# First chunk: slots for all eight q/k tiles, and their transposes in one run behind gate/up group 2

## The chip, the core and the metric

The kernel runs on one core of one Trainium2 chip. A core has a matrix engine (PE, with its weight loads shown as PEld), a vector engine (DVE), a scalar engine (ACT), GpSimd (POOL) and a sync engine (SP), each with an instruction stream of its own, and 16 DMA engines that the streams feed. The metric is the device time of one execution in microseconds (us); lower is better. Before the change the median of three runs is 576.93 us.

## The reference

A sequence of 2048 tokens of width 576 in bf16. The normed input goes through sliding-window attention (32 heads of 18, a window of 256) and through a gated block (width 4608), and the two results are multiplied:

```python
xn = layernorm(x)
qkv = xn @ wqkv                    # 576 x 1728; 32 heads, Dh = 18
mask = (i - j >= 0) & (i - j < 256)
p = softmax(where(mask, q @ k.T * Dh ** -0.5, -1e9))
s = (p @ v).reshape(B, S, D) @ wo
h = sigmoid(xn @ w_gate) * (xn @ w_up)     # width F = 4608
g = silu(h @ w_down)
out = x + s * g
```

## The kernel before

The tokens are cut into four chunks of 512 (`NCH`, `CH`), each of four tiles of 128. A chunk goes through layer norm, the projections to q, k and v, attention interleaved with the gate/up product, the output projection of the attention, and the down projection. The program is built as a list of operations with dependencies; `schedule` (a planner with estimated durations, transfer sizes and priorities) fixes the order on each engine before anything runs, and `emit` writes that order out with semaphore waits. On the chip each engine, SP too, goes through its own list in order; an instruction that has to wait holds up all that stand behind it.

What matters here is the first chunk:

- Projections (`project`, line 448). One q, k or v tile of 128 tokens takes 18 matmuls; the chunk has twelve such tiles, created in the order of `QKV_FIRST` ("q0 q1 v0 v1 q2 v2 k0 v3 k1 q3 k2 k3").
- `build_qk`. A q or k tile is copied from PSUM (q by DVE at line 490, k by ACT at line 491) into one of `RPK` = 3 slots of the buffer `pk`, 32 heads padded to 32 columns each. The padding is zeroed once by `pkz` on ACT (line 323). From the slot a DMA transpose, issued by SP (line 205), puts the tile into `qkp`, from which the scores are computed. A slot is taken again only when its transpose has landed; eight tiles share three slots.
- Gate/up weights (`load9`, line 206). The 4608 columns are cut into 36 tiles and these into 12 groups of three; a group is four DMAs of 240, 192, 192 and 240 KB into one of `RW` = 3 buffers `wgs`. A tile takes 18 matmuls (line 748), a group 54. The buffer of a group is free for the third next one when its last matmul is done.
- Attention (`build_unit`, line 556 for the scores; `build_pv`, line 639). The scores go to PSUM banks 0 to 3, ACT writes their exponentials (line 579) into one of `NEXP` = 5 buffers `expr`, DVE masks them (line 611), and PV reads them. A unit of scores needs the transposed q and k tiles that it multiplies.
- `behind`: an operation with this mark is placed by the planner only after the named one has been placed. Before, the transposes from the third on (`QKT_BEHIND = 2`) stand behind the last DMA of gate/up group 1.

On SP this gives, in order: the x tiles, the weights of q and v, gate/up group 0, the weights of k, two transposes (q0, q1), group 1, one transpose (q2), group 2, two transposes (k0, k1), group 3, three transposes (q3, k2, k3), group 4, and so on. On PE: seven projection tiles, 26 gate/up matmuls, two projection tiles, 36 gate/up, one tile, 36 gate/up, two tiles, 8 gate/up, and the first unit of scores.

Of the kernel before, what the change touches and what calls it, by code (L numbers as in the profile page):

```python
# [10 lines left out]
DH = 18  # L11
F = 4608
P = 128
# [21 lines left out]
RW = 3  # L35
RT = 2
NEXP = 5
RPK = 3
HP = 32
# [31 lines left out]
LATE_SLACK = 5000.0  # L71
LN_STEP = 1
XT_CUT = 4
QKT_BEHIND = 2
WARM = 10
X0_SLACK = 0.0
X_PRIO = (-9, -9, -9, -9)
# [3 lines left out]
W_FACTOR = 1.42  # L81
X0_FACTOR = 1.7
XT_BYTES = 1.2
DMA_LAT_NS = 1600.0
DMA_BYTES_PER_NS = 320.0


def mm_ns(n):
    return max(28.0, n / 2.4 + 2.5)


def act_ns(n):
    return n / 1.2 + 80.0


def dve_ns(n, rate=1.0):
    return n / (0.96 * rate) + 75.0
# [68 lines left out]
class Builder:  # L166
# [16 lines left out]
    def op(self, eng, occ, fn, name, deps=(), prio=3, **kw):  # L183
        o = Op(eng, occ, fn, name, deps, prio, **kw)
        o.cidx = len(self.ops)
        self.ops.append(o)
        return o
# [117 lines left out]
    def build_init(self):  # L305
        op = self.op
        self.op_negh = op("DVE", 60, lambda e: e.memset(self.neghalf[:, :], -0.5), "neghalf", prio=0)
        self.op_pre = op("DVE", 250, lambda e: e.memset(self.hT[:, 0, :], 1.0), "pre", prio=-9)
        id1 = op("POOL", 200, lambda e: e.memset(self.op_[:, NOT - 1, 0:P], 1.0), "id1", prio=0)
        self.op_ident = op("POOL", 300, lambda e: e.affine_select(  # L310
            self.op_[:, NOT - 1, 0:P], self.op_[:, NOT - 1, 0:P], pattern=[[1, P]], compare_op=ALU.is_equal, fill=0.0,
            base=0, channel_multiplier=-1), "id2", deps=[id1], prio=0)
        m1 = op("POOL", 300, lambda e: e.memset(self.m13[:, :, :], 1.0), "m1", prio=1)
        m2 = op("POOL", 300, lambda e: e.affine_select(
            self.m13[:, 0, :], self.m13[:, 0, :], pattern=[[1, P]], compare_op=ALU.is_ge, fill=0.0,
            base=0, channel_multiplier=-1), "m2", deps=[m1], prio=1)
        self.op_mask = op("POOL", 300, lambda e: e.affine_select(
            self.m13[:, 1, :], self.m13[:, 1, :], pattern=[[-1, P]], compare_op=ALU.is_ge, fill=0.0,
            base=-1, channel_multiplier=1), "m3", deps=[m2], prio=1)
        vo1 = op("POOL", 1100, lambda e: e.memset(self.vau[:, :, 0:H, DH:DH + 1], 1.0), "vones", prio=1)  # L320
        self.op_vones = op("POOL", 300, lambda e: e.memset(self.vau[:, :, H, :], 1.0), "vpad", deps=[vo1], prio=1)
        self.warm(WARM, "warm:0", [self.op_pre])
        self.op_pkz = op("ACT", 1300 + 1900, lambda e: e.memzero(self.pk[:, :, :, :]), "pkz", prio=0)

    def warm(self, n, name, deps):
        ps = Psum((3,))
# [4 lines left out]
            return r  # L331
        self.op_warm = self.pe(n * WARM_NS, f, name, deps=deps, prio=-9, psum=[ps])

    def load9(self, low, up, w_low, w_up, name, lane, deps, prio, factor=1.42):
        cols = w_low.shape[1]
        a = w_low.rearrange("(j p) c -> p j c", p=64)
        b = w_up.rearrange("(j p) c -> p j c", p=64)
        out = []
        for k, (dst, src, n) in enumerate(((low[:, 0:5, :], a[:, 0:NC:2, :], 5), (up[:, 0:4, :], b[:, 1:NC:2, :], 4),
                                           (low[:, 5:NC, :], a[:, 1:NC:2, :], 4), (up[:, 4:NC, :], b[:, 0:NC:2, :], 5))):  # L340
            out.append(self.dma(dst, src, factor * n * 64 * cols * 2, f"{name}.{k}", lane + (k,), deps=deps, prio=prio,
                                issue=W_ISSUE_NS))
        return out
# [31 lines left out]
    def build_ln(self, c):  # L375
# [4 lines left out]
        for i in range(QPC):  # L380
# [30 lines left out]
            if c > 0:  # L411
                for k, (i0, i1, col) in enumerate(((0, NKT, 0), (NKT, NC, 64))):
                    o = self.dma(self.xn[:, i0:i1, tok], self.xnr[:, sr, col:col + (i1 - i0) * P],
                                 XT_BYTES * (i1 - i0) * P * P * 2, f"xt:{st}.{k}", ("xt", i, k), deps=[wr, ap] + dxn,
                                 prio=-2, issue=XT_ISSUE_NS, transpose=True)
# [65 lines left out]
            prev = o  # L481

    def build_qk(self, c, i, j, old):
        spk, dpk = self.r_pk.take()
        o, ps = self.project(c, i, j, f"qk:{c}:{i}:{j}", dpk, self.op_pv[c - 1][NHG - 1] if c > 0 else None)

        def f_ev(e):
            dst = self.pk[:, spk, :, 0:DH].rearrange("p (t h) d -> p t h d", t=2)
            if j == 0:
                return e.tensor_copy(dst, self.halves(ps))  # L490
            return e.activation(dst, self.halves(ps), ACTF.Copy)  # L491
        ev = self.rd("ACT" if j else "DVE", act_ns(D) if j else dve_ns(D), f_ev, f"qke:{c}:{i}:{j}",
                     deps=[o, self.op_pkz] + [t for t in (self.op_on[c - 1] if c > 0 else [])], prio=1, psum=[ps])
        c0 = j * CH + i * P
        dm = self.dma(self.qkp[:, :, c0:c0 + P], self.pk[:, spk, :, :].rearrange("p h d -> p (h d)"),
                      XT_BYTES * 8 * P * P * 2, f"qkt:{c}:{i}:{j}", ("qk", i, j), deps=[ev] + old, prio=0,
                      issue=XT_ISSUE_NS, transpose=True)
        self.r_pk.release(spk, dm)
        (self.op_q, self.op_k)[j].append(dm)
        self.op_qkt.append(dm)  # L500
        return o
# [223 lines left out]
    def build_ffn(self, c):  # L725
# [25 lines left out]
        for ft in range(NFT + 1):  # L751
            if ft < NFT:
                if ft % FG == 0:
                    fg = ft // FG
                    sw, dw = self.r_w.take()
                    slots.append(sw)
                    wp = W_PRIO[fg] if c == 0 and fg < RW else -2
                    fc = slice(fg * FG * P, (fg + 1) * FG * P)
                    ws = self.load9(self.wgs[0:64, sw, :, :], self.wgs[64:P, sw, :, :], self.wg[:, fc],
                                    self.wu[:, fc], f"w:{c}:{fg}", ("w", sw),  # L760
                                    dw + ([self.w_gate] if c > 0 and fg < RW else []), wp)
                    dmas.append(ws)
                    if c == 0 and fg == 1:
                        for o in self.op_qkt[QKT_BEHIND:]:
                            o.behind = ws[-1:]
                pg.append(Psum((6,), (7,), (5,), (4,)))
                pu.append(Psum((6,), (7,), (5,), (4,)))
            war = [self.f2_last[ft // WDG]] if self.f2_last and ft < NFT else []

            def f_a(e, ft=ft):  # L770
                for i in range(NA):
                    if ft < NFT:
                        r = step(e, 0, ft, i)
                    if ft > 0:
                        r = step(e, 1, ft - 1, NC - NA + i)
                return r
            oa = self.pe(NA * mm_ns(CH), f_a, f"fa:{c}:{ft}",
                         deps=(dmas[ft // FG] + self.all_xn + war if ft < NFT else []), prio=3,
                         psum=[pg[ft]] if ft < NFT else [], mode="r64", odeps=mms)
            if ft > 0:  # L780
                pu[ft - 1].users.append(oa)
                if ft % FG == 0:
                    self.r_w.release(slots[ft // FG - 1], oa)
                th_mul(ft - 1, ob, oa)
            if ft == NFT:
                break

            def f_b(e, ft, i0, i1):
                for i in range(i0, i1):
                    step(e, 0, ft, NA + i)  # L790
                    r = step(e, 1, ft, i)
                return r
            ob = oa
            for n, (i0, i1) in enumerate(zip(FB_CUTS, FB_CUTS[1:])):
                ob = self.pe((i1 - i0) * mm_ns(CH), lambda e, ft=ft, i0=i0, i1=i1: f_b(e, ft, i0, i1), f"fb{n}:{c}:{ft}",
                             deps=[ob], prio=3, psum=[pu[ft]] if n == 0 else [], mode="r64")
                if n > 0:
                    pu[ft].users.append(ob)
            pg[ft].users.append(ob)
            self.op_f1[(c, ft)] = ob  # L800
            mms = [ob]
# [5 lines left out]
        for blocks in (((0, 1), (2,), (3,)) if c == 0 else ((0,), (1,), (2,), (3,))):  # L807
# [5 lines left out]
            for q in range(NWD):  # L813
                for i in blocks:
                    def f_f2(e, q=q, i=i, ps=banks[i]):
                        b = ps.banks[0] * 512
                        for fl in range(WDG):
                            ft = q * WDG + fl
                            lhsT = self.hT[:, ft, i * P:(i + 1) * P]
                            for n0, n1 in ((0, 512), (512, D)):  # L820
# [3 lines left out]
                    deps = [self.op_hT[ft] for ft in range(q * WDG, (q + 1) * WDG)] + [self.op_wd[q]]  # L824
                    o = self.op("PE", WDG * (mm_ns(512) + mm_ns(64)), f_f2, f"f2:{c * QPC + i}:{q}", deps, 3,
                                alloc=[banks[i]] if q == 0 else [], mode="full",
                                odeps=prev + ([self.op_wop[i - RTH]] if q == 0 and i >= RTH else []))
# [66 lines left out]
    def schedule(self):  # L894
# [46 lines left out]
        while n < total:  # L941
# [37 lines left out]
            if o.lane is not None:  # L979
                free[e] = st + o.occ  # L980
                bs = max(free[e] + DMA_LAT_NS, bw)
                bw = bs + o.nbytes / DMA_BYTES_PER_NS
# [147 lines left out]
```

## Time and profile before

| | |
|---|---|
| median of three runs | 576.93 us (576.13 to 577.06) |
| the profiled execution | 576.29 us |
| its span, first to last instruction | 574.5 us |
| PE busy | 566.0 us (99%) |
| DVE, ACT, POOL busy | 294.1, 300.8, 23.0 us |
| granted clock of PE, mean | 0.998 |
| gate/up matmuls (line 748) | 298.7 us, 2592 |
| down projection (line 821) | 135.0 us, 1080 |
| projections (line 448) | 55.3 us, 864 |

The page shows one profiled execution. Times in its timelines count from the first instruction of the span. In the rows below, a number in square brackets is the idle time of an engine before an instruction, and after the arrow stands what ended it; SPq is SP's queue of DMA issues, and the duration of such a row is the time that SP took to issue the transfer, not that of the transfer. "To landing" counts from the start of the issue to the last semaphore update of the transfer. In a row of windows stand: the window, its length, busy time and number of instructions for PE, PEld, DVE, ACT and POOL, PE's granted clock, the share of the DMA engines' time, and GB/s.

### The profile page before, as it was taken

To read this page: it belongs to the slowest core of one execution; us is meant where nothing else is said; L and a number is where in the kernel's file an instruction comes from. 1 tells how busy PE (TensorE), PEld (TensorE's weight loads), DVE (VectorE), ACT (ScalarE), POOL (GpSimd) and SP (SyncE) were. 2 spreads that over 40 slices of the span, in tenths; PEclk is the share of its full clock that TensorE was granted. 3 is DMA by queue.
4 is the path that set the end of the run, shared out by engine and by line. 5 is a ranking of instruction groups with operands and counts; after the bars stand their busy time and mean duration, and the time that the engine had idled before them with its cause. 6 is when DMAs were issued, how large, how long until landed. Compare 5 with 4: busy or idle time off the path is not lost.

```text
span 574.5 us, 14808 instructions
## 1 busy us (share of the span) xinstructions
PE 566.0 (99%) x6350; PEld 274.7 (48%) x6350; DVE 294.1 (51%) x589; ACT 300.8 (52%) x403; POOL 23.0 (4%) x51
## 2 busy tenths in 40 slices
PE   8999999999999999999999999999999999999996
PEld 5544443457444444455753444344654444444554
DVE  5138877422247886621115888772122677774112
ACT  5357787214448887520307787760242778872201
POOL 3001110000001100000000011000000000000000
PEclk9999999999999999999999999999999999999999
DMA  8999999436935665341793666414479356651010
GB/s 203 200 214 251 224 211 232 88 63 119 198 80 135 146 156 126 79 87 42 140 206 91 146 138 151 106 50 100 56 135 186 84 124 138 134 126 40 1 42 21
DMA packets 124861, 72.82 MB, mean 127 GB/s; under 512 B 53630, under 2 KB 124286, under 8 KB 124798
## 3 DMA queue, kind: packets, MB, share of 16 engines
q1 hardware_dynamic: 124798, 71.90, 58.6%
q8 instruction: 50, 0.82, 0.6%
q14 instruction: 13, 0.11, 0.1%
HBM read 55.22 MB, written 2.36 MB: 100 GB/s over the span
## 4 chain that ended last, share of the span: by engine, by line
PE 95%; SPq 3%; DMA 1%; issue 0%; DVE 0%; ACT 0%
PE ps L748 50%; PE ps L821 23%; PE ps L448 8%; PE ps L556 5%; PE ps L639 4%; PE ps L705 3%; SPq L206 2%; PE ps L851 2%; DMA wgs<-in_B_w_up_dram 1%; SPq L205 1%; DVE thf L884 0%; ACT thf L882 0%; DVE thf L886 0%; DVE xf L888 0%
## 5 line engine op out<-in xcount | busy, mean ns | idle before, releaser
L748 PE MATMUL ps<-xn,wgs 64*128 64x512 bf16 x2592 | 298.7, 377 | 1.2 <-DMA wgs<-in_B_w_up_dram 1.2
L579 ACT ACTIVATE expr<-ps 128x1024 bf16<-128x1024 f32 (+1 forms) x184 | 174.9, 1003 | 45.3 <-PE ps L556 45.3
L748 PEld LDWEIGHTS ps<-xn,wgs 64*128 64x128 bf16 x2592 | 119.5, 94 | 152.3 <-issue 19.1
L821 PE MATMUL ps<-wd_sb,hT 128*128 128x512 bf16 (+1 forms) x1080 | 135.0, 287 | 0.0
L734 ACT ACTIVATE tring<-ps 128x512 bf16<-128x512 f32 x144 | 86.4, 600 | 62.6 <-PE ps L748 61.2
L611 DVE TENSOR_TENSOR expr<-expr,m 128x1024 bf16<-128x1024 bf16 (+1 forms) x152 | 81.9, 571 | 68.6 <-ACT expr L579 68.5
L738 DVE SCALAR_TENSOR_TENSOR hT<-tring,ps 128x512 bf16<-128x512 bf16 x144 | 97.0, 675 | 39.0 <-ACT tring L734 27.7
L821 PEld LDWEIGHTS ps<-wd_sb,hT 128*128 128x128 bf16 x1080 | 68.0, 98 | 66.3 <-issue 3.1
L882 ACT ACTIVATE thf<-ps 128x576 bf16<-128x576 f32 (+2 forms) x17 | 10.6, 622 | 110.6 <-PE ps L821 102.8
L884 DVE SCALAR_TENSOR_TENSOR thf<-thf,ps 128x576 bf16<-128x576 bf16 (+2 forms) x17 | 12.2, 719 | 90.0 <-ACT thf L882 89.9
L448 PE MATMUL ps<-wqkv_sb,xn 64*128 64x288 bf16 x864 | 55.3, 283 | 0.2 <-DMA wqkv_sb<-in_A_wqkv_dram 0.2
L448 PEld LDWEIGHTS ps<-wqkv_sb,xn 64*128 64x128 bf16 x864 | 42.9, 94 | 11.2 <-issue 1.3
L556 PE MATMUL ps<-qkp 18*128 18x384 bf16 (+2 forms) x704 | 36.1, 276 | 1.0 <-issue 1.0
L655 DVE STREAM_TRANSPOSE tf<-ps 128x512 f32<-128x512 f32 x32 | 22.9, 715 | 11.4 <-PE ps L556 9.9
L556 PEld LDWEIGHTS ps<-qkp 18*128 18x128 bf16 x704 | 10.8, 92 | 34.4 <-issue 20.8
L490 DVE CAST pk<-ps 128x576 bf16<-128x576 f32 x16 | 12.1, 756 | 28.8 <-PE ps L448 28.6
L639 PE MATMUL ps<-expr,vau 128*32 128x256 bf16 (+2 forms) x704 | 25.6, 277 | 0.0
L621 POOL COPY qkp<-qkp 128x256 bf16<-128x256 bf16 x24 | 11.5, 479 | 317.0 <-PE ps L556 317.0
L669 DVE STREAM_TRANSPOSE op__63<-pk 128x512 bf16<-128x512 bf16 x32 | 22.7, 708 | 1.1 <-DVE pk L663 0.2
L491 ACT ACTIVATE pk<-ps 128x576 bf16<-128x576 f32 x16 | 10.4, 652 | 22.6 <-PE ps L448 22.6
L639 PEld LDWEIGHTS ps<-expr,vau 128*32 128x32 bf16 x704 | 13.1, 97 | 15.3 <-ACT tring L734 6.8
L705 PE MATMUL ps<-wo_sb,oT 64*128 64x512 bf16 (+1 forms) x288 | 19.2, 283 | 0.0
(39 smaller groups left out, 142.6 us busy)
## 6 DMA issues: line engine op xcount, KB each, us to landing
wgs<-in_B_w_gate_dram SPq DMA_DIRECT2D x48, 240.0 KB, 3.8
wgs<-in_B_w_up_dram SPq DMA_DIRECT2D x48, 240.0 KB, 4.9
wgs<-in_B_w_up_dram SPq DMA_DIRECT2D x48, 192.0 KB, 4.0
wgs<-in_B_w_gate_dram SPq DMA_DIRECT2D x48, 192.0 KB, 4.5
wd_sb<-in_B_w_down_dram SPq DMA_DIRECT2D x9, 576.0 KB, 4.7
xf<-in_A_x_dram SPq DMA_DIRECT2D x18, 144.0 KB, 2.3
out_dram<-xf SPq DMA_DIRECT2D x15, 144.0 KB, 1.8
xr<-in_A_x_dram SPq DMA_DIRECT2D x14, 144.0 KB, 4.1
```

The costliest lines, as they stand in the source:

```text
L448: r = e.matmul(self.bank(ps, HV, hf), self.xn[r0:r0 + 64, k, i * P:(i + 1) * P], self.wqkv_sb[r0:r0 + 64, j, k, :], start=(k == 0), stop=( ...
L556: r = e.matmul(self.ps[:, b:b + n * P], self.qkp[r0:r0 + DH, hg, k0:k0 + P], self.qkp[r0:r0 + DH, hg, q0 * P:(q0 + n) * P], start=True, st ...
L579: return e.activation(self.expr[:, es, 2 * pr:2 * pr + 2, 0:nblk * P], src, ACTF.Exp, scale=SM_SCALE)
L611: return e.tensor_tensor(ap, ap, m, ALU.mult)
L639: r = e.matmul(self.ps[32 * j:32 * j + 32, b + q0 * P:b + (q0 + n) * P], vf[:, v0:v0 + 32], self.expr[:, es, j, pos * P:(pos + n) * P], st ...
L655: t1 = self.rd("DVE", dve_ns(CH), lambda e, ps=ps: e.transpose(tf.rearrange("p g d -> p (g d)"), self.bank(ps)), f"t1:{c}:{hg}", deps=[o_p ...
L669: t2 = self.op("DVE", dve_ns(CH), lambda e, on=on: e.transpose(self.op_[:, hg % NOT, :], on.rearrange("p g d -> p (g d)")), f"t2:{c}:{hg}" ...
L705: r = e.matmul(self.bank(ps2[w], n1 - n0, n), self.oT[r0:r0 + 64, kt, qi * P:(qi + 1) * P], self.wo_sb[r0:r0 + 64, kt, n0:n1], start=(swap ...
L734: return e.activation(self.tring[:, st_, :], self.bank(ps), ACTF.Tanh, scale=0.5)
L738: return e.scalar_tensor_tensor(self.hT[:, ft, :], self.tring[:, st_, :], 1.0, self.bank(ps), ALU.add, ALU.mult)
L748: return e.matmul(self.bank((pg, pu)[gu][ft]), self.wgs[r0:r0 + 64, slots[ft // FG], i, fl * P:(fl + 1) * P], self.xn[r0:r0 + 64, i, :], s ...
L821: r = e.matmul(self.ps[:, b + n0:b + n1], lhsT, self.wd_sb[:, q, fl, n0:n1], start=(ft == 0), stop=(ft == NFT - 1))
```

## The change

Eight q/k tiles of the first chunk get a place each: the first three keep the slots of `pk`, the other five use the first two of the four parts of the five `expr` buffers, which hold no exponentials yet. A second memzero on ACT (`pkz2`) zeroes these parts, since the transpose reads the padding too. The first exponentials that go into an `expr` buffer wait for the transpose that reads it. `QKT_BEHIND` becomes a table: all eight transposes of the first chunk stand behind the last DMA of gate/up group 2. Two sizes that only the planner uses (the transfer time it assumes for these transposes, 1.5 in place of 1.2, and for the first five gate/up groups, 1.5 in place of 1.42) are changed as well; they move instructions, not data.

The order that comes out. SP: k weights, group 1, group 2, eight transposes (q0, q1, q2 from `pk`, then k0, k1, q3, k2, k3 from `expr`), group 3, group 4. PE: eight projection tiles, 8 gate/up matmuls, four projection tiles, 116 gate/up matmuls, a unit of scores (8 matmuls of 256 columns, k2 with q2 and q3), 22 gate/up, scores, 18 gate/up, scores, 24 gate/up, scores, 26 gate/up, and the first PV; from there on PE's order is the same as before. ACT has `pkz2` between `pkz` and its first copy of normed tiles, and the four k copies together. A few of the x and `w_down` loads of the first chunk, and with them DVE's layer norm of the next chunk, come later in their queues.

```diff
--- before.py
+++ after.py
@@ -71,7 +71,7 @@
 LATE_SLACK = 5000.0
 LN_STEP = 1
 XT_CUT = 4
-QKT_BEHIND = 2
+QKT_BEHIND = {2: 0}
 WARM = 10
 X0_SLACK = 0.0
 X_PRIO = (-9, -9, -9, -9)
@@ -81,6 +81,8 @@
 W_FACTOR = 1.42
 X0_FACTOR = 1.7
 XT_BYTES = 1.2
+XT0_BYTES = 1.5
+W0_FACTOR = 1.5
 DMA_LAT_NS = 1600.0
 DMA_BYTES_PER_NS = 320.0
 
@@ -320,7 +322,8 @@
         vo1 = op("POOL", 1100, lambda e: e.memset(self.vau[:, :, 0:H, DH:DH + 1], 1.0), "vones", prio=1)
         self.op_vones = op("POOL", 300, lambda e: e.memset(self.vau[:, :, H, :], 1.0), "vpad", deps=[vo1], prio=1)
         self.warm(WARM, "warm:0", [self.op_pre])
-        self.op_pkz = op("ACT", 1300 + 1900, lambda e: e.memzero(self.pk[:, :, :, :]), "pkz", prio=0)
+        self.op_pkz = [op("ACT", 1300 + 1500, lambda e: e.memzero(self.pk[:, :, :, :]), "pkz", prio=0)]
+        self.op_pkz.append(op("ACT", 2500, lambda e: e.memzero(self.expr[:, :, 0:2, :]), "pkz2", prio=0))
 
     def warm(self, n, name, deps):
         ps = Psum((3,))
@@ -331,7 +334,7 @@
             return r
         self.op_warm = self.pe(n * WARM_NS, f, name, deps=deps, prio=-9, psum=[ps])
 
-    def load9(self, low, up, w_low, w_up, name, lane, deps, prio, factor=1.42):
+    def load9(self, low, up, w_low, w_up, name, lane, deps, prio, factor):
         cols = w_low.shape[1]
         a = w_low.rearrange("(j p) c -> p j c", p=64)
         b = w_up.rearrange("(j p) c -> p j c", p=64)
@@ -481,21 +484,30 @@
             prev = o
 
     def build_qk(self, c, i, j, old):
-        spk, dpk = self.r_pk.take()
+        extra = len(self.op_qkt) - RPK if c == 0 else -1
+        if extra < 0:
+            spk, dpk = self.r_pk.take()
+            pk = self.pk[:, spk, :, :]
+        else:
+            dpk = []
+            pk = self.expr[:, extra, 0:2, :].rearrange("p a (h d) -> p (a h) d", d=HP)
         o, ps = self.project(c, i, j, f"qk:{c}:{i}:{j}", dpk, self.op_pv[c - 1][NHG - 1] if c > 0 else None)
 
         def f_ev(e):
-            dst = self.pk[:, spk, :, 0:DH].rearrange("p (t h) d -> p t h d", t=2)
+            dst = pk[:, :, 0:DH].rearrange("p (t h) d -> p t h d", t=2)
             if j == 0:
                 return e.tensor_copy(dst, self.halves(ps))
             return e.activation(dst, self.halves(ps), ACTF.Copy)
         ev = self.rd("ACT" if j else "DVE", act_ns(D) if j else dve_ns(D), f_ev, f"qke:{c}:{i}:{j}",
                      deps=[o, self.op_pkz] + [t for t in (self.op_on[c - 1] if c > 0 else [])], prio=1, psum=[ps])
         c0 = j * CH + i * P
-        dm = self.dma(self.qkp[:, :, c0:c0 + P], self.pk[:, spk, :, :].rearrange("p h d -> p (h d)"),
-                      XT_BYTES * 8 * P * P * 2, f"qkt:{c}:{i}:{j}", ("qk", i, j), deps=[ev] + old, prio=0,
+        dm = self.dma(self.qkp[:, :, c0:c0 + P], pk.rearrange("p h d -> p (h d)"),
+                      (XT_BYTES if c else XT0_BYTES) * 8 * P * P * 2, f"qkt:{c}:{i}:{j}", ("qk", i, j), deps=[ev] + old, prio=0,
                       issue=XT_ISSUE_NS, transpose=True)
-        self.r_pk.release(spk, dm)
+        if extra < 0:
+            self.r_pk.release(spk, dm)
+        else:
+            self.r_exp.release(extra, dm)
         (self.op_q, self.op_k)[j].append(dm)
         self.op_qkt.append(dm)
         return o
@@ -758,10 +770,11 @@
                     fc = slice(fg * FG * P, (fg + 1) * FG * P)
                     ws = self.load9(self.wgs[0:64, sw, :, :], self.wgs[64:P, sw, :, :], self.wg[:, fc],
                                     self.wu[:, fc], f"w:{c}:{fg}", ("w", sw),
-                                    dw + ([self.w_gate] if c > 0 and fg < RW else []), wp)
+                                    dw + ([self.w_gate] if c > 0 and fg < RW else []), wp,
+                                    W0_FACTOR if c == 0 and fg < 5 else 1.42)
                     dmas.append(ws)
-                    if c == 0 and fg == 1:
-                        for o in self.op_qkt[QKT_BEHIND:]:
+                    if c == 0 and fg in QKT_BEHIND:
+                        for o in self.op_qkt[QKT_BEHIND[fg]:]:
                             o.behind = ws[-1:]
                 pg.append(Psum((6,), (7,), (5,), (4,)))
                 pu.append(Psum((6,), (7,), (5,), (4,)))
```

## The prediction

> **What bounds the kernel now.** I read the page's busy times first, then TensorE's waits, then the window in which these waits lie, then the timelines of PE and SP in it. PE is busy for 566.0 of 574.5 us; every change of time is therefore a change of PE's idle time or of its work.
>
> ```profile
> PE 566.0 (99%) x6350; PEld 274.7 (48%) x6350; DVE 294.1 (51%) x589; ACT 300.8 (52%) x403; POOL 23.0 (4%) x51
> ...
> PE ps L330 <- DVE neghalf L307: 1.5, 1, 1.5
> PE ps L748 <- DMA wgs<-in_B_w_up_dram: 1.2, 1, 1.2
> PE ps L556 <- issue: 1.0, 1, 1.0
> ...
> 11.12:49.64 38.52, 36.37 (x424) 20.62 (x422) 12.41 (x21) 19.65 (x29) 0.56 (x1) 1.00 1.14 218
> ```
>
> The first wait is the start. The other two are in the first chunk: the first gate/up matmul that needs group 1 waits 1.2 us for its weights, and a score matmul waits 1.0 us. Between 11.12 us (first long run of projections) and 49.64 us (first PV) PE is idle for 38.52 - 36.37 = 2.15 us, which is these two. The last figures of that row say that the clock was full and the DMA engines were full too (share 1.14, 218 GB/s).
>
> ```profile
> 11.12 5.69 PE L448 MATMUL ps<-wqkv_sb,xn 64*128 64x288 bf16 x90
> 16.64 2.97 PE L748 MATMUL ps<-xn,wgs 64*128 64x512 bf16 x25
> ...
> 26.02 1.26 PE L748 MATMUL ps<-xn,wgs 64*128 64x512 bf16 x10 [1.19 <-DMA wgs<-in_B_w_up_dram]
> ...
> 39.70 0.40 PE L556 MATMUL ps<-qkp 18*128 18x256 bf16 x8 [0.97 <-issue]
> ```
>
> ```profile
> 12.70 1.38 SPq L206 DMA_DIRECT2D wqkv_sb<-in_A_wqkv_dram  x1
> 14.12 3.97 SPq L205 DMA_TRANSPOSE qkp<-pk  x2
> 18.14 0.60 SPq L206 DMA_DIRECT2D wgs<-in_B_w_gate_dram  x1
> ...
> 25.16 0.62 SPq L206 DMA_DIRECT2D wgs<-in_B_w_up_dram  x1
> 25.82 4.84 SPq L205 DMA_TRANSPOSE qkp<-pk  x2
> 30.70 0.60 SPq L206 DMA_DIRECT2D wgs<-in_B_w_gate_dram  x1
> ...
> 33.33 5.59 SPq L205 DMA_TRANSPOSE qkp<-pk  x3
> 38.96 0.60 SPq L206 DMA_DIRECT2D wgs<-in_B_w_gate_dram  x1
> ```
>
> SP issues everything in order. Two transposes (3.97 us) stand ahead of weight group 1, so its last part, issued at 20.11, lands 5.57 us later at 25.68, 0.34 us before PE goes on. The seventh transpose starts inside the run of three at 34.71 and lands 4.9 us later at 39.6: that is what the score of 39.70 waited for, though the view calls it "issue".
>
> **What is removed.** In the new order groups 1 and 2 follow the k weights directly and all eight transposes come after them. Group 1 is then early (below), so the 1.19 us goes. All twelve projections stand ahead of the gate/up work but for eight matmuls, so the slots no longer tie k and q3 to earlier transposes, and the first score moves behind 124 gate/up matmuls. The work between first projections and first PV is the same: 180 projections, 214 gate/up and 28 score matmuls. Fewer changes between projection and gate/up runs save 0 to 0.4 us (10 matmuls after the stall took 1.26 us, against 3.88 us for 36 in the chain of waits); I take 0.2.
>
> **What is added.** A second memzero on ACT, 2560 words a row against the 1536 that took 1.48 us: 2.5 us from 3.56 to about 6.0. ACT's next work starts at 6.43 behind an idle time of 2.87 us, so it costs nothing, with 0.4 us in hand; uncovered it would cost at most 2.5 us.
>
> **When PE needs what, if nothing stalls.** 90 projections took 16.64 - 11.12 = 5.52 us, 0.0613 each; gate/up matmuls take 3.88/36 = 0.108. So 108 projections end at 17.74, 8 gate/up at 18.60, 72 projections at 23.02, 116 gate/up at 35.54: the first score. The score (0.40), 22 gate/up (2.48 in the chain) and the next score (0.33) end at 38.75. Group 1 was needed at the 52nd gate/up matmul, and a group is 54, so groups 2 and 3 are needed at the 106th (33.6) and the 160th. The latter is 14 after that second score, with 0.1 for the change of mode: 40.35.
>
> **When the transfers land.** The k weights land at 12.70 + 5.7 = 18.4, and with 0.34 of hand-over PE could begin them at 18.7: 0.1 us late (0 to 0.5).
> Groups 1 and 2, then: 884.7 KB each at 218 GB/s are 4.06 us, so at the earliest 18.4 + 8.1 = 26.5. At the latest: before, the stretch from 18.4 to the landing of group 2 (25.16 + 6.0 = 31.1) also carried three transposes, whose landings lie at least 0.8 us apart, so 31.1 - 2.4 = 28.7. I take the middle, 27.6. Group 1 is there by about 23, needed at 23.02 + 44 x 0.108 = 27.8.
> The transposes: SP is held back when a transpose follows a full queue. The fifth one of before, issued at 27.35, took 3.30 us to 30.65, though its tile had been evicted at 22.72; that is 0.5 us before the weights ahead of it landed. So the second transpose of the run ends its issue at 27.6 - 0.5 = 27.1, and six more follow. Runs with little else in the queue show their pace:
>
> ```profile
> L205 SPq DMA_TRANSPOSE qkp<-pk x6: 1308/1330/1542, 128.2 to 138.4; - x6
> ...
> L205 SPq DMA_TRANSPOSE xn<-xnr x8: 1262/1272/2397, 111.5 to 121.8; - x8
> ```
>
> 1.33 us and 0.02 to 0.04 between give 1.35 each, 8.1 us; and a run of eight had one of 2.40, 1.1 more than its median. I take half of that, 0.5 (0 to 1.1). The run ends at 35.7. The seventh (the k tile that the first score needs) starts two issues earlier, at 33.0 or so, and lands 3.2 us on at 36.2: the first score is some 0.7 us late.
> Group 3 stands behind all eight; its buffer is free long before (its last reader is the 52nd gate/up matmul). From first issue to last landing group 4 took 6.8 us (38.96; 40.94 + 4.8) and group 3 took 7.1 us (30.70; 32.67 + 5.1). So 35.7 + 6.9 + 0.34 = 42.9 us, where PE wants it at 40.35: **2.6 us late in all**, in which the first score's 0.7 is contained. Queued behind that matmul are the next score and everything after it.
> Two scores now stand 18 gate/up matmuls apart where 22 was the least; ACT's exponentials between them (1.94 us) and a tanh (0.60) need 2.54 us against 18 x 0.108 + 0.4 = 2.35, 0.2 us, but group 3's wait falls into this interval and covers it. Later groups: group 4 is issued 2.7 us behind group 3, lands by about 46 and is needed 54 matmuls after 42.9, at 49: in time. From the first PV on PE's order is unchanged.
>
> **The sum.** -2.15 - 0.2 + 0.1 + 2.6 = +0.35 us on a span of 574.5. The profiled execution took 576.29 us, 1.8 more than its span; the median of the runs shown is 576.93, and on it the forecast is **577.3 us**: the two stalls are moved into one.
>
> **The rivals.**
> *Holes closed.* Group 3 is in time and only the gain is left: -2.15 - 0.2 + 0.1 + 0.2 (ACT) = -2.05, 574.9 us. For it: landings of neighbouring transposes lie 0.8 us apart (31.9 and 32.7), so the DMA engines could take the six in 4.8 us instead of 8.1, and with groups 1 and 2 at 26.5 another 1.1 us; each alone takes most of the 2.6 us away, together all. Against it: no transpose in the profile was issued in less than 1.23 us, so SP sets the pace.
> The Trainium skill ("DMA: Bandwidth & Descriptors", section "Issuing engines are not separate DMA queues") says that the sequencer's time to start a DMA is usually small beside the DMA itself; by that rule this rival would be the forecast, and the rows above speak against it for transposes.
> *Run held up (slower).* At one place: SP between the second and the eighth transpose. One more hold as at 27.35 or 34.71 (3.30 and 2.86 us, 1.5 to 2.0 over the median, against the 0.5 taken) puts group 3 at 44.2 us: +0.35 + 1.3 = +1.65, 578.6 us. It decides when the last transpose is issued after 36.5 us. For it: the DMA engines are full in this stretch. Against it: by then only transposes are queued.
> *Not as described.* The order of instructions does show eight transposes in one run behind group 2, so this rival has no chance of its own.
>
> **Chances.** A measurement of this kernel (runs from 576.13 to 577.06) tells about 0.2%, 1.15 us, from no change. Forecast, within 575.8 to 578.1: 0.42. Holes closed or most of it: 0.27, faster. Run held up: 0.31, slower. The forecast's own range is 575.8 to 578.1. With groups 1 and 2 at 26.5 and no hold the sum is -1.25, and with 28.7 and a full hold of 1.1 it is +2.05; leaving a tenth on each side, the rivals included, gives **575.0 to 578.8**.
>
> **What would show it.** Right: no wait at the 52nd gate/up matmul; eight transposes on SP from about 22, the last issued near 35 us; a wait of PE for group 3's weights of 1 to 2.5 us near 41 us, after a short one at the first score; PE's idle time up to the first PV near 2.3 us. Wrong: group 3 landing before 40 us (then 575), the second transpose issued well before 27 us, or a wait of ACT or DVE on PE in place of these.

## The result, and the profile after

The changed kernel takes 575.85 us (median of 17 runs, 575.27 to 576.53) against 577.08 us (17 runs, 576.13 to 577.90): a ratio of 0.998, 95% interval 0.9973 to 0.9988, or 1.2 us less. The forecast was 577.3 us. The profiled execution of the changed kernel took 575.74 us with a span of 574.0 us; that of the kernel before took 576.29 us with a span of 574.5.

The page's busy times, and TensorE's waits (total, times, longest, in us):

```profile
PE 566.3 (99%) x6350; PEld 273.6 (48%) x6350; DVE 293.9 (51%) x589; ACT 303.0 (53%) x404; POOL 23.4 (4%) x51
...
PE ps L333 <- DVE neghalf L309: 1.5, 1, 1.5
PE ps L760 <- DMA wgs<-in_B_w_up_dram: 1.2, 1, 1.2
```

PE's work is the same to 0.3 us and ACT has about 2 us more of it, the second memzero. Of the two waits in the first chunk one is left. The line is the same as before (748 has become 760), but it is another wait, as the timeline of PE shows:

```profile
17.86 1.24 PE L760 MATMUL ps<-xn,wgs 64*128 64x512 bf16 x8
19.24 4.59 PE L451 MATMUL ps<-wqkv_sb,xn 64*128 64x288 bf16 x72
23.65 12.75 PE L760 MATMUL ps<-xn,wgs 64*128 64x512 bf16 x116
36.34 0.40 PE L568 MATMUL ps<-qkp 18*128 18x256 bf16 x8
...
42.32 0.61 PE L760 MATMUL ps<-xn,wgs 64*128 64x512 bf16 x4 [1.16 <-DMA wgs<-in_B_w_up_dram]
...
49.07 0.68 PE L651 MATMUL ps<-expr,vau 128*32 128x384 bf16 x16
```

The run of 116 gate/up matmuls goes through without a gap, so group 1 and group 2 were there, and the first score follows it at once. Group 3's first matmul waits 1.16 us. A second loss shows only in the starting times: the eight gate/up matmuls begin at 17.86 and the k projections 1.38 us later, where eight of them need 0.88 (in the profile of *g3_mid_again* below, from 17.98 to 18.86). The other 0.50 us is a wait for the k weights, which landed at 19.11. The view shows 0.14 of it as idle time: it counts from the modelled end of the last matmul (19.10), and a matmul's modelled end lies later than the start of the next.

SP's timeline has the reason for the wait at group 3:

```profile
19.32 8.06 SPq L207 DMA_TRANSPOSE qkp<-pk  x3
27.42 7.27 SPq L207 DMA_TRANSPOSE qkp<-expr  x5
34.74 0.60 SPq L208 DMA_DIRECT2D wgs<-in_B_w_gate_dram  x1
...
36.71 0.62 SPq L208 DMA_DIRECT2D wgs<-in_B_w_up_dram  x1
```

The eight transposes hold SP from 19.32 to 34.70. Only then is group 3 issued; the chain of waits gives its last part 5.36 us to landing, 36.71 to 42.07, and PE goes on 0.25 us later. One by one the eight issues took 4.09, 2.58, 1.31, 1.34, 1.34, 1.34, 1.78 and 1.31 us: the first two are held while the weights ahead of them land (the second ends at 26.02, the last part of group 2 lands at 26.44).

From the first PV on the time is the same: from there to the end of the span it is 524.90 us in the profile before and 524.97 after.

### The profile page after: what moved, and what is told of

Read it like the earlier page. It is cut to its first block, busy times and chain, and to the rows that moved or that the text cites. A ratio compares the mean times of both kernels' runs of the same rounds, so it can differ in the third digit from the quotient of the medians.

```text
span 574.0 us, 14808 instructions
## 1 busy us (share of the span) xinstructions
PE 566.3 (99%) x6350; PEld 273.6 (48%) x6350; DVE 293.9 (51%) x589; ACT 303.0 (53%) x404; POOL 23.4 (4%) x51
## 4 chain that ended last, share of the span: by engine, by line
PE 95%; SPq 2%; DMA 2%; issue 0%; DVE 0%; ACT 0%
PE ps L760 50%; PE ps L834 23%; PE ps L451 8%; PE ps L568 5%; PE ps L651 4%; PE ps L717 3%; SPq L208 2%; PE ps L864 2%; DMA wqkv_sb<-in_A_wqkv_dram 1%; DMA wgs<-in_B_w_up_dram 1%; DVE thf L897 0%; ACT thf L895 0%; DVE thf L899 0%; DVE xf L901 0%
## 5 line engine op out<-in xcount | busy, mean ns | idle before, releaser
L568 PE MATMUL ps<-qkp 18*128 18x128 bf16 (+2 forms) x704 | 36.1, 275 | 0.0
L499 DVE CAST pk<-ps 128x576 bf16<-128x576 f32 x15 | 11.3, 756 | 27.8 <-PE ps L451 27.8
L500 ACT ACTIVATE pk<-ps 128x576 bf16<-128x576 f32 x12 | 7.8, 652 | 18.6 <-PE ps L451 18.6
```

Source lines behind the costliest of these rows:

```text
L568: r = e.matmul(self.ps[:, b:b + n * P], self.qkp[r0:r0 + DH, hg, k0:k0 + P], self.qkp[r0:r0 + DH, hg, q0 * P:(q0 + n) * P], start=True, st ...
```

## The experiments

Each ratio is to the kernel before, run beside it, with a 95% interval; medians are in us.

### Does it repeat: after_again, before_again, before_third

The two kernels unchanged, profiled again.

> The changed kernel as it is. Theory A (the end of the first chunk is set by SP: group 3 can only be issued when the eighth transpose is): a wait of PE for group 3 of 0.8 to 1.6 us near 41 us and one of about 0.5 us for the k weights, 0.998 of before, as seen. Rival B (the median's gain of 1.2 us, against 0.5 us between the two profiled spans, comes from something outside the first 50 us): the time from the first PV to the end is shorter than the 524.9 us of before by 0.5 us or more.

Measured: 576.01 (574.97 to 576.34), ratio 0.9974 (0.9965 to 0.9983). The wait for group 3 is 1.47 us, the first score waits 0.18 for the transposes, and the k projections begin 1.06 us after the eight gate/up matmuls, 0.18 more than these need: the k weights landed at 18.46, so this wait is nearly gone. PE goes on with group 3 at 42.25 and comes to the first PV at 49.00, each within 0.1 us of the first profile. Theory A held but for the size of the wait for the k weights; from the first PV to the end it is 524.96 us, so B fell.

> The kernel before, once more, for a second profile beside its median. The profiled execution shown before took 576.29 us where the median is 577.1. Theory A (the rest of the median's gain is in the same two waits, which were short in that one execution): the waits for group 1 and at the second score sum to 2.5 to 3.2 us here. Rival B (it lies elsewhere): they are 2.2 us again, and the time from the first PV to the end is over 525.4 us.

Measured: 576.91 (576.48 to 578.11), ratio 0.9998 (0.9989 to 1.0006); the profiled execution took 577.42. Its waits:

```profile
PE ps L556 <- issue: 1.5, 1, 1.5
PE ps L748 <- DMA wgs<-in_B_w_up_dram: 1.5, 1, 1.5
```

At two decimals 1.49 and 1.45, together 2.94 us, where the profile that I had summed has 2.15. From first PV to end it is 524.90 us again, so nothing behind it differs between these two executions; theory B fell.

> The kernel before, a third profile of it. Theory A (the two waits of the profile that I summed, 1.19 + 0.97 us, were short ones; the repeat had 1.45 + 1.49): their sum is again above 2.4 us, and the first PV begins after 49.9 us. Theory B (they scatter about 2.15 us and the repeat was the exception): the sum is at or under 2.3 us and the first PV begins at 49.4 to 49.8 us.

Measured: one run, 576.94. The waits that answer to the two:

```profile
PE ps L556 <- issue: 1.4, 1, 1.4
...
PE ps L748 <- ACT tring L734: 0.8, 1, 0.8
```

They sum to 2.17 us, as theory B has it. (The second is named after ACT; group 1 landed at 25.70 and PE went on at 25.95.) The first PV nevertheless begins at 49.98, as theory A has it, so neither held whole: the first long run of projections began at 11.44 instead of 11.12, 0.32 us late, and the rest of the stretch is as long as in the first profile. So executions of the kernel before differ by some 0.8 us in these waits and some 0.3 us in the start; the one first profiled was short in both.

### Slots without the new order: slots_only

```diff
-QKT_BEHIND = {2: 0}
+QKT_BEHIND = {1: 2}
```

> One edit: the eight slots stay, and the order of SP goes back to transposes from the third on behind group 1 (two ahead of group 1, two behind it, four inside group 2). Theory A (SP's order is what sets the waits; the slots only make an order possible): the wait for group 1 is back (0.5 to 1.2 us) and group 2, with six transposes ahead of most of it, is late by 1.5 to 3 us: 577 to 579 us. Rival E (the slots are what helps, by freeing the k and q3 projections): no slower than the changed kernel, 575.9 us.

Measured: 579.83 (577.75 to 580.78), ratio 1.0041 (1.0026 to 1.0057), slower than the kernel before.

```profile
PE ps L760 <- DMA wgs<-in_B_w_up_dram: 1.7, 1, 1.7
...
PE ps L568 <- ACT expr L591: 1.2, 1, 1.2
...
PE ps L568 <- DMA qkp<-expr: 0.9, 1, 0.9
```

With the slots free, projections and scores come earlier in PE's order, and the transposes stand ahead of group 2 on SP. Three waits follow: for group 2 (landed at 38.60), for a transpose, and for exponentials, where two scores stand only 8 gate/up matmuls apart. The wait for group 1 that theory A expected did not come: it landed at 26.34, and PE, with all twelve projections done first, came to it only at some 28.0.

A fourth loss stands in no list of waits. Behind the three waits, the 18 gate/up matmuls from 38.74 take 3.56 us where 18 at 0.108 take 1.94, 1.6 us more, and in the row of windows the granted clock is 0.57:

```profile
38.74:42.30 3.56, 3.56 (x19) 1.35 (x20) 1.63 (x3) 0.29 (x1) 0.00 (x0) 0.57 1.00 214
```

Before it, from 33.00 to 38.74, PE was busy for 1.97 of 5.74 us. That this idle time is what lowered the clock is likely, but no run tests it. The one of the seven executions whose mean clock was 1.000 took 577.75 us; the six others, at 0.992 to 0.997, took 578.91 to 580.78. So theory A's direction held, with a median above its range; E fell. The slots by themselves gain nothing; of the 2.4 us that they cost, the larger part probably goes with the lower clock.

### The order without the slots: order_only

The kernel before with its three slots, and its transposes behind group 2.

```diff
-QKT_BEHIND = 2
+QKT_BEHIND = 0
...
-                    if c == 0 and fg == 1:
+                    if c == 0 and fg == 2:
```

> The kernel before with one edit of its order: all transposes behind group 2, with three slots in place of eight. The ring of slots then cuts the run in three (three, three, two) with groups 3 and 4 between them. Theory A: groups 1 and 2 are early, group 3 has only three transposes ahead of it and lands by 36 us, where it is needed near 41; at most 1 us of waits at the projections of k0 to q3, which need the slots of the first three: 1.2 to 2.2 us faster than before, so at least as fast as the changed kernel. Rival E (the slots are needed): slower than the changed kernel by 0.5 us or more, with waits of PE at projections for landings of transposes.

Measured: 577.55 (576.62 to 578.37), ratio 1.0006 (0.9997 to 1.0014): no difference.

```profile
PE ps L448 <- DMA qkp<-pk: 1.4, 2, 1.1
...
PE ps L748 <- ACT tring L734: 0.6, 1, 0.6
```

The wait at group 1 has shrunk to 0.64 us, but two projections wait 1.40 us for a slot, that is, for a transpose to land. Theory A's time was missed and E's held. Together with *slots_only*: each half moves the waits to another place or adds some, and only the two together take some away.

### The planner's sizes: plan_old

```diff
-XT0_BYTES = 1.5
-W0_FACTOR = 1.5
+XT0_BYTES = 1.2
+W0_FACTOR = 1.42
```

> One edit: the planner's two new sizes are put back (1.2 and 1.42), which moves the first score from behind 124 to behind 106 gate/up matmuls and nothing on SP up to group 4. Theory A: the first score waits 1 to 1.5 us for the seventh transpose, and group 3, which lands at the same time as before that edit (42 us), is then waited for the less: the same time as the changed kernel within 0.4 us. Rival F (the new sizes are what helps): 1 us or more slower.

Measured: 576.38 (575.68 to 576.94), ratio 0.9982 (0.9974 to 0.9991), about the time of the changed kernel, whose interval it overlaps.

```profile
PE ps L568 <- DMA qkp<-expr: 1.3, 1, 1.3
...
PE ps L451 <- DMA wqkv_sb<-in_A_wqkv_dram: 0.7, 1, 0.7
```

The first score is placed earlier and meets the seventh transpose, which lands at 36.19; behind that wait group 3 is in time. (The wait for the k weights, which landed at 19.68 here, is there too.) The delay is taken at one place or the other, and SP's run of transposes sets both. Theory A roughly held, F fell.

### What is left of the wait: k_first, g3_mid, k_and_g3

*k_first* issues the k weights ahead of gate/up group 0, so that all twelve projections come before the first gate/up matmul:

```diff
-QKV_LOAD = (-8, -4, -6)
+QKV_LOAD = (-8, -5.5, -6)
```

> One edit: the k weights are loaded ahead of gate/up group 0, so all twelve projections run in one piece. Theory A: the 0.5 us at the k weights is gone, but group 3 lands no earlier (near 42 us), so PE waits for it 0.5 us longer: the same time as the changed kernel within 0.3 us. Rival C (the two waits are independent and add up): 0.5 us faster than the changed kernel, the wait for group 3 stays at 1.2 us.

Measured: 575.47, ratio 0.9967 (0.9954 to 0.9980). No wait for the k weights; the wait for group 3 is 0.90 us, since group 3 landed at 41.42, and the first PV begins at 48.46. Theory A's longer wait did not come; rival C's 0.5 us is near the 0.4 measured, though its wait of 1.2 us is shorter here. The gain over the changed kernel of about 0.4 us lies inside the intervals.

*g3_mid* puts group 3 between the fifth and the sixth transpose:

```diff
-QKT_BEHIND = {2: 0}
+QKT_BEHIND = {2: 0, 3: 5}
```

> One edit: the last three transposes stand behind group 3 in place of ahead of it, and the planner moves the first score behind 160 gate/up matmuls. Theory A: group 3 is issued from about 30 us, lands by 38 us, the wait of 1.2 us is gone and nothing takes its place: 1.0 to 1.3 us faster than the changed kernel, about 574.7 us. Rival D (the DMA engines are full, so whatever is moved ahead makes something else late): a wait of about the same length at the first score or at group 4, the same time within 0.4 us.

Measured: 574.76, ratio 0.9954 (0.9937 to 0.9971).

```profile
23.98 16.64 PE L760 MATMUL ps<-xn,wgs 64*128 64x512 bf16 x152
40.61 0.40 PE L568 MATMUL ps<-qkp 18*128 18x256 bf16 x8
```

Group 3 is issued from 31.07 and lands at 38.92; PE has no wait for it and none new. The planner has also moved the first score behind 160 gate/up matmuls in place of 124, but group 3 is needed behind 160 gate/up matmuls in both orders (here at 40.94), so what serves it is the earlier landing. Theory A held, D fell.

*k_and_g3* has both edits:

> Both edits. Theory A: with group 3 out of the way the 0.5 us of the k weights counts too: 1.5 to 1.8 us faster than the changed kernel, 2.7 to 3.0 us faster than before, about 574.1 us. Rival D: no faster than the changed kernel by more than 0.5 us.

Measured: 574.75, ratio 0.9955 (0.9939 to 0.9971), with no wait of PE between 11.3 us and the first PV, and a span of 572.6 against 573.3 of *g3_mid*, but the same median: theory A's further 0.5 us is not in it, and D fell.

The two were run again to tell whether the k weights count. (The expectations have one thing the wrong way round: five transposes stand ahead of group 3 and three behind it.)

> The changed kernel with three transposes ahead of group 3 and five behind it, once more, beside the one that also has the k weights earlier. Both theories: 574.4 to 575.1 us, no wait of PE for group 3. Theory A (the wait for the k weights, 0.45 us in its profile, is on the path): it is 0.3 to 0.7 us slower than k_and_g3_again. Theory B (the time that the k weights save is lost again before the end, or the wait is not there in most executions): the two agree within 0.2 us.

> The changed kernel with the k weights issued earlier and three transposes ahead of group 3, once more. Theory A (the wait for the k weights counts): 574.0 to 574.5 us, 0.3 to 0.7 us faster than g3_mid_again. Theory B (it does not): 574.4 to 575.0 us, within 0.2 us of g3_mid_again. Both: no wait of PE over 0.2 us between the start and the first PV.

Measured: *g3_mid_again* 574.65 (5 runs, 574.46 to 575.33), ratio 0.9955 (0.9941 to 0.9969); *k_and_g3_again* 575.21 (12 runs, 574.31 to 577.03), ratio 0.9967 (0.9956 to 0.9979). Theory A, that the earlier k weights gain 0.3 to 0.7 us, fell: the kernel that has them is not the faster one, and the intervals overlap. B's first reason, that time is lost later, shows in the profile of *k_and_g3_again*, an execution of 576.08 us. PE has no wait over 0.2 us up to the first PV at 51.42, and then two, in its timeline:

```profile
54.96 1.26 PE L760 MATMUL ps<-xn,wgs 64*128 64x512 bf16 x10 [0.55 <-DMA wgs<-in_B_w_up_dram]
...
84.63 2.12 PE L760 MATMUL ps<-xn,wgs 64*128 64x512 bf16 x18 [0.38 <-DMA wgs<-in_B_w_up_dram]
```

From the first PV to the end it is 522.58 us, against 521.08 in *k_and_g3*. Nothing ties this loss to the earlier k weights: *k_and_g3* is the same kernel and has no such waits. SP's loads between 50 and 80 us differ in the same way, first for *k_and_g3_again*, then for *k_and_g3* (an execution of 574.50 us), from issue to landing:

```profile
DMA to landing us min/median/max: 8.5/10.3/11.5
```

```profile
DMA to landing us min/median/max: 3.7/7.2/9.8
```

B's second reason shows too: in *g3_mid_again* the k projections begin at 18.86, right behind the eight gate/up matmuls, so in that execution there was no wait for the k weights to remove. How often either happens these profiles don't tell. What the four runs do show is that putting group 3 among the transposes beats the kernel before, by 1.9 to 2.5 us. Three of them also lie 1.1 to 1.2 us under the changed kernel; the fourth, *k_and_g3_again*, lies 0.6 under it, with an interval that overlaps.

## Why the prediction was wrong

It was right about what happens, two stalls that become one behind SP's run of transposes, and wrong about the size of that one and about the sum: I had a loss of 0.35 us, and 1.2 us were gained. The time lay at the very edge of the forecast's own range (575.8 to 578.1) and 0.95 us above the rival *Holes closed*, whose condition, group 3 in time, was not met.

**What held.** Both stalls are gone. *Second memzero*: 2.32 us, 3.47 to 5.79, and ACT was idle for 0.69 us before its next work, so the cover held. *Six transposes in 8.1 us and a hold of 0.5*: the last six took 26.07 to 34.70, 8.63 us, and in *after_again* 9.04. Each has one hold, 0.4 and 0.9 us longer than the other issues. That half of 1.1 us lies between the two was luck; what the hold goes with stands in the last section. *Second transpose issued 0.5 us before group 2 lands*: 0.4 us and 0.23. *Group 3 in 6.9 us*: 7.33 and 6.80. *First score 0.7 late*: not so here, where the seventh transpose landed at 35.53 and PE came at 36.34; 0.18 in *after_again*. *Group 4*: landed at 46.11, no wait. *Score gap*: covered by the wait for group 3, as said; *slots_only* shows what such a gap costs uncovered, 1.16 us at 8 matmuls.

**What isn't shown: "fewer changes, 0.2".** Between the first long run of projections and the first PV, PE took 36.37 us without the waits before and 36.18 after (49.07 - 11.23 - 1.16 - 0.50), 0.19 less. But this takes the wait for the k weights from starting times and the others as idle time; with its idle time of 0.14 it is 36.54 after, 0.17 more. The rows that the term was taken from don't carry it either: the 1.26 us of the ten matmuls runs to the end of the last one, and the next run begins 1.08 us after the first of them, 0.108 for each, as in the run of 36. So the 0.19 below is a remainder and not a saving that was seen.

**What failed: "2.6 us late in all".** PE waited 1.16 us at group 3, and 1.47 in *after_again*. From one profile to the other the terms are now -2.15 (stalls), -0.19 (remainder), +0.50 (k weights), +1.16 (group 3) and +0.11 (the projections began at 11.23 instead of 11.12), together -0.57: the first PV moved from 49.64 to 49.07. Against +0.35 that is 0.92 us, from two steps:

- *Groups 1 and 2 by 27.6.* They landed at 26.44. I gave them 9.2 us behind the k weights, and took 8.1 for the least that the rate of 218 GB/s allows. They took 7.33 us here, 7.85 in *after_again*, and from 6.9 to 7.9 in the seven other profiles in which they follow one another; on average 7.4, or 1769 KB at some 240 GB/s. My rate was that of a stretch in which transposes and weights alternate. The upper bound had the same fault: I took the three transposes in it at 0.8 us each, the least distance of two landings; 12.7 us for the stretch less 7.4 for the weights leaves 5.3, some 1.8 each. The k weights landed 0.7 us later than I had it (19.11 against 18.4), and group 3 took 0.4 us longer from its first issue, which gave part of it back. In all PE went on with group 3 at 42.32 instead of 42.95: 0.63 us.
- *The sum.* The other 0.29 us I made in adding. The wait for the k weights lies ahead of the wait for group 3 and only shortens it; I counted its 0.1 beside the 2.6. And the timeline "if nothing stalls", from which the 2.6 was measured, ran 0.2 us ahead of the sum it was put into (its 116 gate/up matmuls take 12.52 us, and they took 12.69): 40.35 and the 6.75 us from group 3 to the first PV (42.32 to 49.07) are 47.10, where 49.64 - 2.15 - 0.2 is 47.29. Going on directly from 42.95 with 6.75 would have given 49.70, no change at all.

**The step from the profile to the median.** 577.3 to 575.85 is 1.45 us; 0.92 is accounted for, and about 0.5 is left. I put the difference on the median, as if the two stalls were in every execution as long as in this one. The profiled execution was 0.64 us under its median, and that of the changed kernel 0.11 under its own: 0.53. The two repeats of the kernel before show where this can lie: 2.94 us of waits in one, 0.8 more than in the profile that I summed, and a start 0.32 us later in the other. How often each happens in the 17 executions behind the median isn't known.

**The rivals.** *Holes closed* rested on transposes going faster than SP's pace. They don't: the last six took 8.63 us to issue, and eight landings lie between 27.39 and 36.63, 1.32 us apart on average, which is the time of an issue. (Behind the late fifth they land 0.88 and 0.85 us apart, so it is the issues that set the pace.) The Trainium skill ("DMA: Bandwidth & Descriptors", "Issuing engines are not separate DMA queues") has the time to start a DMA as usually small beside the DMA itself; the trace agrees for the weights (0.62 us to issue, 4 to 8 to landing, four parts in 2.6 us against some 3.7 for a group to pass) and not for a run of these transposes. Of the 2.6 us, 1.16 are left. Of the rest, 0.63 went because PE could go on earlier, with the weights ahead of the run landing sooner, and 0.81 only because PE came there later, at 41.16 in place of 40.35, which is no gain. *Run held up* did not come: the last issue ended at 34.70 and 35.16, before the 36.5 from which it decides.

**Still open.** Whether the k weights cost anything in the median, and what makes the start and the landings of one kernel differ by some tenths of a microsecond between executions.

## What to carry to other kernels

Transfers of one kind in a row are no measure for mixed ones, nor the other way round: before moving a block of weights ahead of a run of transposes, take its pace from a stretch that holds weights alone. Waits that follow one another on the same engine are not added; carry one timeline through to the point where the order is the same again, and compare that. And where the gain is two stalls of a microsecond, see them in more than one execution before setting them against a median: here they were 2.2 us in two and 2.9 in another.

## What the runs showed of the hardware

- Two weight groups behind one another pass at some 240 GB/s; in the order before, with three transposes (787 KB) among them, the same stretch moved 2556 KB in 12.7 us, 201 GB/s.
- Within the run of transposes one landing comes late: the fifth, 2.97 us after the fourth (30.83 to 33.80), and 2.70 in *after_again*, though it was issued 1.39 us after it. In all eight profiles in which the run stands behind groups 1 and 2 with the new slots it is 2.6 to 3.2. In each of them a load of 16 KB of instructions passes between the two landings; the profile of the changed kernel has it at 31.90, for 0.89 us, in the view of DMA queues from 31.5 to 32.5:

```profile
q8 instruction: 1, 0.02, 5.6%
```

- This holds for all transposes of the 13 profiles. Of 503 pairs issued within 4.2 us of one another, 83 land more than 2.1 us apart, and each of these has an instruction load in the gap or less than 1 us before it; the 420 others have none and land at most 2.03 us apart. The long issues go with it: 1.78 us in the run after, 2.20 in *after_again*, and the 2.40 of the kernel before from which the prediction took its hold (114.11, with a load from 113.9). No run moves such a load, so that it is the cause is not shown.
- In *slots_only* the granted clock was 0.57 from 38.74 to 42.30, behind 5.74 us in which PE was busy for 1.97; gate/up matmuls went at about half their pace. No other profile here has such a stretch.
- Between two executions of one kernel, with the same order of instructions, the loads from 50 to 80 us took 10.3 and 7.2 us to land in the median; the former cost two waits on PE that the latter does not have.
